# Attention scores with the array's row halves on two heads of a pair, queries turned once, keys and values in plain order

## The chip, the core and the metric

The kernel runs on one core of a Trainium2 chip. The metric is device time in microseconds. TensorE is called PE below; its weight loads are the rows PEld. DVE is VectorE, ACT is ScalarE, POOL is GpSimd, and SP is the queue that issues nearly all DMAs.

## The reference

What matters here is the attention part; two feed-forward blocks on its result follow.

```python
def _attn_ref(q, k, v, w1, b1, w2):          # batch 2, heads 8, seq 576, head_dim 64, all float32
    scores = scale * np.matmul(q, k.transpose(0, 1, 3, 2))
    ...
    h = np.maximum(x @ w1 + b1, 0.0)         # x: a function of the two positions
    bias = h @ w2                            # one number for each head and pair of positions
    scores = scores + bias.transpose(2, 0, 1)[None, :, :, :]
    attn = np.exp(scores - np.max(scores, axis=-1, keepdims=True))
    attn = attn / (np.sum(attn, axis=-1, keepdims=True) + 1e-09)
    return np.matmul(attn, v)
```

## The kernel before

The queries of both batches are cut into nine tiles of 128 rows (`TILES`; the seventh, `COMB`, holds the last 64 rows of both batches). A tile has four pairs of heads, so that there are 36 units u = 4t + p, and the attention part is a pipeline over these 36 units. For each unit:

- `scores` (line 442, written S.u in the table) multiplies the turned queries by the turned keys. A head has only 64 dimensions, so one product fills 64 of the array's 128 rows. Before the change the lower 64 rows take the even keys of a head and the upper 64 rows its odd keys. For this the raw keys are loaded as pairs of neighbouring rows (512 bytes in one piece), and the queries are loaded twice into the two halves of a tile, so that each turned tile of queries holds the same head in both halves.
- `softmax_d` (line 455, on DVE) adds the bias and takes the row's extreme; it writes the tile `e` with the keys back in plain order, which is a step of two elements. `softmax_a` (line 466, on ACT) takes the exponential.
- `e_turn` (T.u.0 to T.u.2) turns `e` on PE, 128 columns at a time, nine times in a unit, into the PSUM tile `tps`; eight of the nine read every second column (`e[:, o:o + 255:2]`), the ninth reads 128 columns in a row. `e_copy` brings the result to SBUF on ACT or DVE.
- `pv` (PV.u, line 504) multiplies by the values.

Ahead of and between these stand the turning of keys (kT) and queries (`q_turn`, qT.t.0 and qT.t.1: four transposes each into `qps`, then `q_copy` on ACT) and the bias groups (B.n). A bias group is made of `bias_R` (R, mostly on DVE), `bias_mm` (`bps`, PE), `bias_evac` (`ev`, ACT and DVE), `bias_store` to DRAM (`biasd`), and later `bias_load` back into the tile `bias`. Weights of the feed-forward part come as `raw`, are converted by ACT (line 145) and DVE (lines 153, 154, 158) in `wm`, split into `wh` and `wl` (lines 137 and 166), and wait there for their use.

PE's order in this part is the written table `ORDER`. The order on the other engines and on the DMA queue is chosen by the scheduler when the kernel is built; it follows the planner's keys and the space that is free in SBUF. Each engine and the queue of SP run in order: an instruction that waits holds back all that stand behind it. PSUM has two buffers for scores (`ps_s`) and three for everything that is turned (`ps_t`).

Of the kernel before, what the change touches and what calls it, by code (L numbers as in the profile page):

```python
# [10 lines left out]
F32 = mybir.dt.float32  # L11
F32R = mybir.dt.float32r
I32 = mybir.dt.int32
ACTF = mybir.ActivationFunctionType
# [25 lines left out]
kT.0,0,0 B.16 B.17 B.18 kT.0,1,0 B.19 kT.0,2,0 qT.0.0 B.21 B.22 B.23 B.20 S.0 B.13 B.12 B.11 B.10 B.9 qT.0.1 kT.0,1,1  # L40
B.8 kT.0,0,1 qT.1.0 S.1 T.0.0 B.14 T.0.2 S.2 kT.1,0,0 T.1.0 T.0.1 kT.1,0,1 B.15 T.1.2 S.3 T.1.1 T.2.0 kT.1,1,0 B.24
kT.1,1,1 T.2.2 S.4 T.2.1 PV.0 PV.1 B.25 T.3.0 T.3.2 S.5 PV.2 qT.2.0 qT.1.1 B.26 T.3.1 T.4.0 rps.0 T.4.2 S.6 B.27 B.28
PV.3 T.4.1 T.5.0 T.5.2 S.7 PV.4 T.5.1 T.6.0 T.6.2 S.8 PV.5 B.29 B.30 qT.3.0 T.7.0 qT.2.1 T.7.2 T.6.1 S.9 PV.6 T.7.1
T.8.0 rps.1 T.8.2 S.10 T.8.1 B.32 B.31 PV.7 T.9.0 B.33 PV.8 T.9.1 T.9.2 S.11 T.10.0 T.10.2 S.12 T.11.0 qT.3.1 qT.4.0
B.34 PV.9 T.10.1 T.11.2 S.13 PV.10 B.35 T.11.1 T.12.0 B.0 rps.2 T.12.2 T.13.0 S.14 PV.11 T.12.1 T.13.2 S.15 T.14.0
T.14.2 B.2 B.1 PV.12 T.14.1 T.13.1 S.16 PV.13 B.3 T.15.0 qT.5.0 qT.4.1 T.15.2 S.17 B.4 PV.14 T.15.1 T.16.0 rps.3
T.16.2 S.18 B.5 PV.15 T.16.1 T.17.0 T.17.2 S.19 PV.16 T.17.1 T.18.0 B.7 T.18.2 B.6 S.20 PV.17 T.19.0 qT.6.0 qT.5.1
T.18.1 T.19.2 S.21 PV.18 T.19.1 T.20.0 rps.4 T.20.2 S.22 PV.19 T.20.1 T.21.0 T.21.2 S.23 PV.20 T.21.1 T.22.0 T.22.2
S.24 PV.21 T.22.1 T.23.0 qT.7.0 qT.6.1 T.23.2 S.25 PV.22 T.23.1 T.24.0 rps.5 T.24.2 S.26 PV.23 T.24.1 T.25.0 T.25.2
S.27 PV.24 T.25.1 T.26.0 T.26.2 S.28 PV.25 T.26.1 T.27.0 qT.8.0 qT.7.1 T.27.2 S.29 PV.26 T.27.1 T.28.0 rps.6 T.28.2  # L50
S.30 PV.27 T.28.1 T.29.0 T.29.2 S.31 PV.28 T.29.1 T.30.1 T.31.0 T.30.0 T.30.2 S.32 PV.29 qT.8.1 T.31.2 S.33 PV.30
# [14 lines left out]
def kernel(ctx, tc, q, k, v, w1, b1, w2, w_in, w_out, w_gate, w_val, w_out2, rms_g, dtab, ntab, itab, out):  # L66
# [170 lines left out]
    if True:  # L237
# [27 lines left out]
        kS = [p.tile([128, H, SH], F32, name=f"kS{b}") for b, p in enumerate((kp0, kp1))]  # L265
        vs = [p.tile([128, 2, H, 2, D], F32, name=f"vs{b}") for b, p in enumerate((vp0, vp1))]
# [7 lines left out]
        pairs = lambda x: x.rearrange("h (p r) d -> p h (r d)", r=2)  # L274

        def load_q(t, hh):

            if hh == 0:
                raw_t["q", t] = rawp.tile([128, H, 2, D], F32, tag="rawq", name="rawq", bufs=BUFS["rawq"])
            h = slice(4 * hh, 4 * hh + 4)  # L280
            for z in range(2):
                a = raw_t["q", t][:, h, z, :]
                if t == COMB:
                    for b in range(B):
                        nc.sync.dma_start(out=a[64 * b:64 * b + 64], in_=q[b, h, 512:576, :].rearrange("h s d -> s h d"))
                else:
                    b, c = TILES[t]
                    nc.sync.dma_start(out=a, in_=q[b, h, c * 128:(c + 1) * 128, :].rearrange("h s d -> s h d"))

        def load_k(b, blk, hh):  # L290

            a = rawp.tile([128, 4, 2, D], F32, tag="rawk", name="rawk", bufs=BUFS["rawk"])
            if blk == 2:
                for o in range(4):
                    src = k[o // 2, 4 * (o % 2):4 * (o % 2) + 4, 512:576, :]
                    nc.sync.dma_start(out=a[32 * o:32 * o + 32].rearrange("p h r d -> p h (r d)"), in_=pairs(src))
            else:
                nc.sync.dma_start(out=a.rearrange("p h r d -> p h (r d)"), in_=pairs(k[b, 4 * hh:4 * hh + 4, 256 * blk:256 * blk + 256, :]))
            raw_t["k", b, blk, hh] = a
# [13 lines left out]
        def turn_four(a, name):  # L313
            ps = ps_t.tile([128, 4, 128], F32, tag="t", name=name)
            for x in range(4):
                transpose(ps[:, x, :], a[:, x].rearrange("p z d -> p (z d)"))
# [619 lines left out]
```

## Time and profile before

| | |
|---|---|
| median of three runs (lowest, highest) | 646.02 us (645.57, 646.43) |
| span of the profiled execution | 646.5 us |
| attention part, from the start to the first `h` matmul of the feed-forward part | 210.5 us |
| feed-forward part | 436.0 us |
| PE busy over the span | 623.6 us (96%) |
| DVE busy | 460.9 us (71%) |
| ACT busy | 340.9 us (53%) |
| mean granted clock of PE | 0.997 |

The profiled execution has no row outside its span, and the span is as long as the slowest of the three runs (0.1 us apart); so its rows can be read against a time of 646.5 us, 0.5 us over the median.

### The profile page before, as it was taken

How to read it: one execution, taken by the hardware profiler on the slowest of the kernel's cores; microseconds unless marked ns; L12 is line 12 of the kernel's file. 1: busy time of each engine (PE TensorE's matmuls, PEld its weight loads, DVE VectorE, ACT ScalarE, POOL GpSimd, SP SyncE). 2: the span in 40 equal slices, each digit the busy share in tenths (PEclk: the TensorE clock that was granted, in tenths of full speed). 3: DMA queues.
4: the chain of work that ended last, by engine and by line, in shares of the span. 5: the costliest groups of instructions: out<-in, count | busy, mean ns of one | idle time of the engine just before them, and what ended most of it. 6: DMA issues, size and time to landing. Idle time of an engine off the chain costs nothing.

```text
span 646.5 us, 10976 instructions
## 1 busy us (share of the span) xinstructions
PE 623.6 (96%) x4172; PEld 527.6 (82%) x4172; DVE 460.9 (71%) x852; ACT 340.9 (53%) x700; POOL 143.8 (22%) x114
## 2 busy tenths in 40 slices
PE   4889999998999999999999999999999999999997
PEld 2346666676688999999999989999899999999996
DVE  6887788646764899888843799969776761387812
ACT  4867676776766555555534556564444441253511
POOL 1000111001210243333310023323332330033400
PEclk9999999998999999999999999999999999999999
DMA  6899647478500254433320123433434340154301
GB/s 161 273 316 279 178 144 187 116 154 248 200 2 1 71 158 132 131 121 122 119 62 1 34 98 131 131 130 99 138 123 127 103 152 11 34 179 147 98 0 50
DMA packets 74721, 80.16 MB, mean 124 GB/s; under 512 B 23980, under 2 KB 59436, under 8 KB 74668
## 3 DMA queue, kind: packets, MB, share of 16 engines
q1 hardware_dynamic: 74404, 79.38, 41.6%
q8 instruction: 33, 0.54, 0.3%
q14 instruction: 20, 0.16, 0.1%
q10 hardware_dynamic: 264, 0.07, 0.0%
HBM read 66.19 MB, written 13.25 MB: 123 GB/s over the span
## 4 chain that ended last, share of the span: by engine, by line
PE 86%; DVE 5%; DMA 4%; ACT 3%; issue 1%; SPq 0%; ACTq 0%; DVEq 0%
PE h L726 39%; PE ya L771 18%; PE yb L771 9%; PE pv L504 5%; PE tps L101 5%; PE s L442 4%; PE bps L372 3%; DVE e L455 2%; DVE R L359 1%; ACT e L466 1%; DMA raw<-in_moe_w_in_dram 1%; DMA bias<-biasd 1%; ACT ev L395 1%; DMA biasd<-ev 1%; PE qps L101 1%
## 5 line engine op out<-in xcount | busy, mean ns | idle before, releaser
L166 POOL TENSOR_TENSOR wl<-wm,wh 128x512 fp32r<-128x512 f32 x85 | 125.9, 1481 | 305.3 <-ACT wh L137 187.6
L158 DVE SCALAR_TENSOR_TENSOR wm<-raw,wm 128x512 int32<-128x512 int32 x85 | 121.7, 1431 | 1.0
L735 ACT CAST gh<-r 128x384 fp32r<-128x384 f32 x84 | 43.2, 514 | 115.9 <-DVE r L758 69.0
L726 PE MATMUL h<-nh,wh 128*128 128x384 f32 x288 | 97.3, 338 | 0.0
L726 PE MATMUL h<-nh,wl 128*128 128x384 f32 x288 | 96.7, 336 | 0.0
L726 PE MATMUL h<-nl,wh 128*128 128x384 f32 x288 | 96.5, 335 | 0.0
L466 ACT ACTIVATE e<-e,m 128x576 f32<-128x576 f32 x72 | 55.5, 771 | 35.2 <-DVE m L455 35.0
L726 PE MATMUL h<-xh,wh 128*128 128x384 f32 x192 | 65.4, 340 | 0.0
L758 DVE TENSOR_TENSOR r<-r,h 128x384 f32<-128x384 f32 x36 | 19.9, 553 | 63.2 <-PE h L726 63.2
L726 PE MATMUL h<-xh,wl 128*128 128x384 f32 x192 | 64.7, 337 | 0.0
L726 PE MATMUL h<-xl,wh 128*128 128x384 f32 x192 | 64.5, 336 | 0.0
L154 DVE SCALAR_TENSOR_TENSOR wm<-raw,wm 128x512 int32<-128x512 int32 x85 | 60.3, 710 | 2.8
L455 DVE CUSTOM_DVE_ANT_1 e<-s,bias 128x576 f32<-128x576 f32 x72 | 52.4, 757 | 10.4 <-PE s L442 7.9
L145 ACT ACTIVATE wm<-raw 128x512 f32<-128x512 f32 x85 | 57.0, 671 | 3.4 <-DMA raw<-in_moe_w_in_dram 2.7
L738 DVE TENSOR_TENSOR gl<-r,gh 128x384 fp32r<-128x384 f32 x84 | 46.6, 555 | 16.8 <-ACT gh L735 16.8
L726 PEld LDWEIGHTS h<-nh,wh 128*128 128x128 f32 x288 | 54.1, 188 | 2.3 <-DVE nl L835 0.9
L726 PEld LDWEIGHTS h<-nl,wh 128*128 128x128 f32 x288 | 54.1, 188 | 1.4
L359 DVE TENSOR_SCALAR R<-T,NB 128x320 f32<-128x320 f32 (+17 forms) x124 | 49.9, 457 | 7.2 <-PE bps L372 7.0
L101 PE MATMUL tps<-ident,e 128*128 128x128 f32 x324 | 53.0, 297 | 1.7 <-ACT et L486 1.2
L726 PEld LDWEIGHTS h<-nh,wl 128*128 128x128 f32 x288 | 54.0, 188 | 0.0
L101 PEld LDWEIGHTS tps<-ident,e 128*128 128x128 f32 x324 | 41.5, 201 | 14.2 <-issue 6.9
L746 ACT ACTIVATE r<-h,half_c 128x384 f32<-128x384 f32 x48 | 27.7, 577 | 47.7 <-PE h L726 47.7
(95 smaller groups left out, 1092.3 us busy)
## 6 DMA issues: line engine op xcount, KB each, us to landing
raw<-in_moe_w_out_dram SPq DMA_DIRECT2D x33, 512.0 KB, 3.6
biasd<-ev SPq DMA_DIRECT2D x36, 295.5 KB, 3.5
raw<-in_moe_w_in_dram SPq DMA_DIRECT2D x18, 512.0 KB, 3.7
raw<-in_moe_w_gate_dram SPq DMA_DIRECT2D x18, 512.0 KB, 3.6
bias<-biasd SPq DMA_DIRECT2D x15, 576.0 KB, 4.9
raw<-in_moe_w_val_dram SPq DMA_DIRECT2D x16, 512.0 KB, 3.6
rawq<-in_q_dram SPq DMA_DIRECT2D x32, 128.0 KB, 4.1
bias<-biasd SPq DMA_DIRECT2D x10, 288.0 KB, 3.8
```

Of the source, the lines that this page charges most:

```text
L101: nc.tensor.transpose(out, in_, ident[:n, :n])
L145: nc.scalar.activation(out=m, in_=raw[:, :, 1].bitcast(F32), func=ACTF.Abs, scale=2.0 ** -112)
L154: nc.vector.scalar_tensor_tensor(out=m, in0=raw[:, :, 0], scalar=29, in1=m, op0=ALU.logical_shift_right, op1=ALU.bitwise_or,)
L158: nc.vector.scalar_tensor_tensor(out=m, in0=raw[:, :, 1], scalar=-0x80000000, in1=m, op0=ALU.bitwise_and, op1=ALU.bitwise_or,)
L166: nc.gpsimd.tensor_tensor(out=lo, in0=m, in1=hi, op=ALU.subtract)
L359: nc.vector.tensor_scalar(out=R, in0=src, scalar1=NB1[:, col], scalar2=None, op0=ALU.max)
L455: nc.vector.tensor_tensor_reduce(out=e_t[u][:, a, :].rearrange("p (j r) -> p r j", r=2), in0=s[:, :, :SH], in1=bt[u][:, a, :].rearrange("p ...
L466: nc.scalar.activation(out=e_t[u][:, a, :], in_=e_t[u][:, a, :], func=ACTF.Exp, scale=-1.0, bias=m_t[t][:, h:h + 1], accum_out=sum_t[t][:, ...
L726: nc.tensor.matmul(ps, lhsT=w[wz][:, c * 128:(c + 1) * 128], rhs=x[xz][:, c, :], start=(i == 0), stop=(i == 11),)
L735: nc.scalar.copy(out=gh, in_=g)
L738: nc.vector.tensor_tensor(out=gl, in0=g, in1=gh, op=ALU.subtract)
L771: nc.tensor.matmul(y_t[ph, n, t], lhsT=g[gz][:, t * 128:(t + 1) * 128], rhs=w[wz], start=(f == 0 and i == 0), stop=(f == F - 1 and i == 2),)
```

## The change

- Scores: the lower 64 rows of the array take the first head of a pair, the upper 64 rows the second; each product covers the first or the second half of the keys (z). The four products of a unit now run over z first and over the two heads inside, so that both score buffers are taken from the start and each is complete only with the third and fourth product.
- Queries: one load of 256 KB and one `q_turn` of four transposes for a tile in place of four loads of 128 KB and two turns of four.
- Keys and values: loaded in plain order, in pieces of 256 bytes in place of 512, with twice as many DMAs for the large blocks.
- `e` is written and read in plain order: all transposes of `e_turn` read 128 columns in a row.
- `ORDER` loses qT.t.1 for each tile; all that is left keeps its place. The planner's numbers stay.

```diff
-T.14.2 B.2 B.1 PV.12 T.14.1 T.13.1 S.16 PV.13 B.3 T.15.0 qT.5.0 qT.4.1 T.15.2 S.17 B.4 PV.14 T.15.1 T.16.0 rps.3
+T.14.2 B.2 B.1 PV.12 T.14.1 T.13.1 S.16 PV.13 B.3 T.15.0 qT.5 T.15.2 S.17 B.4 PV.14 T.15.1 T.16.0 rps.3
...
-        kS = [p.tile([128, H, SH], F32, name=f"kS{b}") for b, p in enumerate((kp0, kp1))]
-        vs = [p.tile([128, 2, H, 2, D], F32, name=f"vs{b}") for b, p in enumerate((vp0, vp1))]
+        kS = [p.tile([128, 4, S], F32, name=f"kS{b}") for b, p in enumerate((kp0, kp1))]
+        vs = [p.tile([128, 4, H, D], F32, name=f"vs{b}") for b, p in enumerate((vp0, vp1))]
...
+        def load_q(t):
+
+            a = raw_t["q", t] = rawp.tile([128, H, D], F32, tag="rawq", name="rawq", bufs=BUFS["rawq"])
+            if t == COMB:
+                for b in range(B):
+                    nc.sync.dma_start(out=a[64 * b:64 * b + 64], in_=rows(q[b, :, 512:576, :]))
+            else:
+                b, c = TILES[t]
+                nc.sync.dma_start(out=a, in_=rows(q[b, :, c * 128:(c + 1) * 128, :]))
...
-                nc.sync.dma_start(out=a.rearrange("p h r d -> p h (r d)"), in_=pairs(k[b, 4 * hh:4 * hh + 4, 256 * blk:256 * blk + 256, :]))
+                a = rawp.tile([128, 2, 4, D], F32, tag="rawk", name="rawk", bufs=BUFS["rawk"])
+                for c in range(2):
+                    r0 = 256 * blk + 128 * c
+                    nc.sync.dma_start(out=a[:, c], in_=rows(k[b, 4 * hh:4 * hh + 4, r0:r0 + 128, :]))
...
-                for blk in range(2):
-                    r0 = 64 * o + 256 * blk
-                    nc.sync.dma_start(out=vs[b][:, blk, o::2].rearrange("p h r d -> p h (r d)"), in_=pairs(v[b, o::2, r0:r0 + 256, :]))
+                for x in range(4):
+                    r0 = 64 * o + 128 * x
+                    nc.sync.dma_start(out=vs[b][:, x, o::2], in_=rows(v[b, o::2, r0:r0 + 128, :]))
...
-        def q_turn(t, hh):
-            ps_of["q", t, hh] = turn_four(raw_t["q", t][:, 4 * hh:4 * hh + 4], "qps")
-
-        def q_copy(t, hh):
-            if hh == 0:
-                q_t[t] = [qp.tile([128, 4, 128], F32, tag=f"q{z}", name=f"q{z}") for z in range(2)]
-            nc.scalar.activation(out=q_t[t][hh], in_=ps_of["q", t, hh], func=ACTF.Copy, scale=0.125)
+        def q_turn(t):
+            ps_of["q", t] = turn_four(raw_t["q", t], "qps")
+
+        def q_copy(t):
+            q_t[t] = qp.tile([128, 4, 128], F32, tag="q", name="q")
+            nc.scalar.activation(out=q_t[t], in_=ps_of["q", t], func=ACTF.Copy, scale=0.125)
...
             for a in range(2):
-                h = 2 * p + a
-                s = ps_s.tile([128, 2, 512], F32, tag="s", name="s")
+                ps_of["s", u, a] = ps_s.tile([128, 2, 512], F32, tag="s", name="s")
+            for z in range(2):
                 for b, sl in cols:
-                    for r in range(2):
-                        rows = slice(64 * r, 64 * r + 64)
+                    for a in range(2):
+                        half = slice(64 * a, 64 * a + 64)
                         nc.tensor.matmul(
-                            s[sl, r, :SH], lhsT=q_t[t][h // 4][rows, h % 4, sl], rhs=kS[b][rows, h, :], start=True, stop=True,
+                            ps_of["s", u, a][sl, z, :SH], lhsT=q_t[t][half, p, sl], rhs=kS[b][half, p, z * SH:z * SH + SH],
+                            start=True, stop=True,
                         )
...
-                out=e_t[u][:, a, :].rearrange("p (j r) -> p r j", r=2),
+                out=e_t[u][:, a, :].rearrange("p (z j) -> p z j", z=2),
...
-                o = (0, 640, 512)[part] + 256 * (x // 2) + x % 2
-                transpose(ps[:, x, :], e[:, o:o + 128] if part == 2 else e[:, o:o + 255:2])
+                o = (0, 640, 512)[part] + 128 * x
+                transpose(ps[:, x, :], e[:, o:o + 128])
...
-                            lhsT, rhs = vs[b][:, x // 2, 2 * p + a, x % 2, :], et[:, 4 * a + x, sl]
+                            lhsT, rhs = vs[b][:, x, 2 * p + a, :], et[:, 4 * a + x, sl]
```

How the built program moves, at three places. First PE between the scores S.8 and S.9 (`qps` are turned queries, `tps` turned `e`). Before:

```order
L372 MATMUL bps<-R,W2b 32x480 x4
L372 MATMUL bps<-R,W2b 32x496 x4
L101 MATMUL qps<-ident,rawq 128x128 x4
L101 MATMUL tps<-ident,e 128x128 x4
L101 MATMUL qps<-ident,rawq 128x128 x4
L101 MATMUL tps<-ident,e 128x128 x5
L442 MATMUL s<-kS_136,q_787 128x288 x4
```

PE in the changed kernel at the same place:

```order
L370 MATMUL bps<-R,W2b 32x480 x4
L370 MATMUL bps<-R,W2b 32x496 x4
L101 MATMUL qps<-ident,rawq 128x128 x4
L101 MATMUL tps<-ident,e 128x128 x9
L440 MATMUL s<-kS_136,q 128x288 x4
```

One group of four query transposes is gone, and nothing else has moved on PE, here or elsewhere in the program.

Second DVE after the softmax step of u = 8 (the ISA rows are `softmax_d`; R makes bias rows). Before:

```order
L359 TENSOR_SCALAR R<-T,NB_114 128x528 x4
L393 TENSOR_SCALAR ev<-bps,INV 128x95
L359 TENSOR_SCALAR R<-T,NB_114 128x544
L486 COPY et<-tps 128x128
L359 TENSOR_SCALAR R<-T,NB_114 128x544 x2
L455 ISA e,m<-s,bias 128x2x288
```

DVE in the changed kernel at the same place:

```order
L357 TENSOR_SCALAR R<-T,NB_114 128x528 x4
L153 TENSOR_SCALAR wm<-wm 128x512
L391 TENSOR_SCALAR ev<-bps,INV 128x95
L154 SCALAR_TENSOR_TENSOR wm<-raw,wm 128x512
L484 COPY et<-tps 128x128
L357 TENSOR_SCALAR R<-T,NB_114 128x544 x3
L158 SCALAR_TENSOR_TENSOR wm<-raw,wm 128x512
L453 ISA e,m<-s,bias 128x576
```

The conversion of the first feed-forward weight now stands here, and those of the next two stand within the two units that follow (u = 9 and 10); before, the first four stood around u = 24 to 28, and the changed kernel has its fourth at u = 22. Their `raw` loads on SP and their first step on ACT (line 145) have moved with them: the smaller query tiles leave room in SBUF, so that the scheduler can place `raw` and `wm` before the bias tiles are freed.

Third SP at the first bias loads (`bias` is what the first softmax steps wait for; `rawk` are keys). Before:

```order
L401 DMA biasd_71<-ev 16x8x591 x2
L427 DMA bias<-biasd_72 128x576 x2
L427 DMA bias<-biasd_72 128x2x576
L298 DMA rawk<-in_k_dram 128x4x128
L427 DMA bias<-biasd_72 128x2x576 x2
```

SP in the changed kernel at the same place:

```order
L399 DMA biasd_71<-ev 16x8x591 x2
L425 DMA bias<-biasd_72 128x576
L296 DMA rawk<-in_k_dram 128x4x64 x2
L425 DMA bias<-biasd_72 128x576
L425 DMA bias<-biasd_72 128x2x576 x3
```

A block of keys, now in two DMAs, stands ahead of the second half of the bias for u = 0 and of the bias for u = 1; it stood behind both.

## Rows read from the trace of the kernel before

**Rows 1.** Busy time by stage: us, PE, PEld, DVE, ACT, POOL, clock, DMA share, GB/s.

```profile
0.00:42.00 42.00, 28.26 (x211) 12.62 (x213) 30.72 (x88) 26.62 (x60) 2.33 (x13) 1.00 0.85 245
42.00:85.00 43.00, 42.25 (x405) 28.43 (x401) 34.76 (x91) 31.64 (x73) 2.70 (x3) 1.00 0.80 215
85.00:104.00 19.00, 18.91 (x198) 12.48 (x196) 14.83 (x40) 13.59 (x30) 2.09 (x2) 1.00 0.72 202
104.00:147.00 43.00, 42.96 (x437) 30.43 (x437) 28.68 (x77) 30.63 (x70) 4.06 (x5) 1.00 0.60 141
147.00:180.00 33.00, 29.57 (x366) 22.52 (x363) 23.52 (x53) 22.98 (x53) 7.38 (x7) 0.95 0.69 213
180.00:210.50 30.50, 30.50 (x336) 24.64 (x334) 16.28 (x43) 18.93 (x44) 3.17 (x3) 1.00 0.00 1
210.50:646.50 436.00, 431.19 (x2232) 396.49 (x2232) 312.13 (x465) 196.47 (x374) 122.11 (x82) 1.00 0.32 100
```

**Rows 2.** Chain that ended last, by line: 85 to 105 us, then 147 to 178 us.

```profile
by line: DVE R L359 16.2%; ACT ev L395 13.8%; ACT e L466 11.9%; DMA rawq<-in_q_dram 10.4%; DVE e L455 10.0%; issue 6.6%; DVE et L486 6.0%; PE bps L372 5.5%; ACT q L340 5.4%; PE s L442 3.8%; SPq L401 2.6%; DVE ev L393 2.5%; ACT rt L528 2.2%;
...
by line: DMA raw<-in_moe_w_in_dram 21.7%; DVE e L455 11.8%; PE s L442 9.1%; PE pv L504 8.2%; ACT e L466 8.1%; DVE wm L154 7.5%; issue 5.1%; PE tps L101 4.8%; DVE et L486 4.5%; PE qps L101 4.2%; DVE wm L158 4.2%; DVE wm L153 3.3%; ACT et L48
```

**Rows 3.** PE timeline: start us, us, operation, count (`qps` queries, `tps` turned `e`).

```profile
54.67 1.09 PE L101 MATMUL qps<-ident,rawq 128*128 128x128 f32 x8
...
121.64 1.22 PE L101 MATMUL tps<-ident,e 128*128 128x128 f32 x8
```

**Rows 4.** Line 101 alone: count, ns min/median/max, first and last start.

```profile
L101 PEld LDWEIGHTS tps<-ident,e x324: 138/209/219, 32.0 to 208.1; 128*128 128x128 f32 x162
L101 PEld LDWEIGHTS qps<-ident,rawq x72: 137/141/153, 15.0 to 191.8; 128*128 128x128 f32 x72
L101 PE MATMUL qps<-ident,rawq x72: 272/273/329, 15.1 to 191.9; 128*128 128x128 f32 x72
```

**Rows 5.** Chain at the start (a DMA), and DVE's first wait for u = 1 (timeline).

```profile
27.62 6.32 DMA bias<-biasd
...
34.07 0.76 DVE L455 CUSTOM_DVE_ANT_1 e<-s,bias 128x576 f32<-128x576 f32 x1 [1.55 <-DMA bias<-biasd]
```

**Rows 6.** Stretches of value loads, then query loads: us, POOL, clock, DMA share, GB/s.

```profile
45.00:47.00 2.00, 0.04 (x1) 1.00 1.12 261
...
51.00:53.00 2.00, 0.00 (x0) 1.00 1.05 197
```

**Rows 7.** Chain (first row) and timeline, 146 to 161 us, around the first `raw` load.

```profile
146.01 6.72 DMA raw<-in_moe_w_in_dram
...
149.80 1.20 PE L442 MATMUL s<-kS,q 64*64 64x288 f32 x16
...
150.94 1.09 PE L504 MATMUL pv<-et,vs 128*64 128x128 f32 x16
...
152.91 0.69 ACT L145 ACTIVATE wm<-raw 128x512 f32<-128x512 f32 x1 [2.73 <-DMA raw<-in_moe_w_in_dram]
...
156.16 0.66 PE L101 MATMUL qps<-ident,rawq 128*128 128x128 f32 x4 [2.32 <-ACT et L486]
...
156.91 1.71 PE L442 MATMUL s<-kS,q 64*64 64x288 f32 x16
...
158.54 1.97 PE L504 MATMUL pv<-et,vs 128*64 128x128 f32 x16
```

**Rows 8.** DVE: two steps of a weight's conversion (timeline), and its busy time 72 to 96 us.

```profile
153.63 0.43 DVE L153 TENSOR_SCALAR wm<-wm 128x512 int32<-128x512 int32 x1 [2.28 <-ACT wm L145]
...
155.37 0.69 DVE L158 SCALAR_TENSOR_TENSOR wm<-raw,wm 128x512 int32<-128x512 int32 x1
...
72.00:96.00 24.00, 18.71 (x49) 1.00 0.47 132
```

**Rows 9.** Timeline: exponential of u = 17, and the turning that reads it.

```profile
120.60 0.76 ACT L466 ACTIVATE e<-e,m 128x576 f32<-128x576 f32 x1
...
126.76 1.33 PE L101 MATMUL tps<-ident,e 128*128 128x128 f32 x9
```

More of the change, by code (lines that the diff above doesn't have):

```diff
@@ L39 @@
 ORDER = """
[L40 to L44, printed above, removed]
+kT.0,0,0 B.16 B.17 B.18 kT.0,1,0 B.19 kT.0,2,0 qT.0 B.21 B.22 B.23 B.20 S.0 B.13 B.12 B.11 B.10 B.9 kT.0,1,1
@@ L271 @@
         copy = lambda e: {"A": nc.scalar.copy, "D": nc.vector.tensor_copy, "P": nc.gpsimd.tensor_copy}[e]
-        pairs = lambda x: x.rearrange("h (p r) d -> p h (r d)", r=2)
-        def load_q(t, hh):
-            if hh == 0:
[L279 to L288, printed above, removed]
+        rows = lambda x: x.rearrange("h s d -> s h d")
@@ L293, in load_k @@
             if blk == 2:
-                for o in range(4):
-                    src = k[o // 2, 4 * (o % 2):4 * (o % 2) + 4, 512:576, :]
-                    nc.sync.dma_start(out=a[32 * o:32 * o + 32].rearrange("p h r d -> p h (r d)"), in_=pairs(src))
-            else:
-                nc.sync.dma_start(out=a.rearrange("p h r d -> p h (r d)"), in_=pairs(k[b, 4 * hh:4 * hh + 4, 256 * blk:256 * blk + 256, :]))
+                a = rawp.tile([128, H, D], F32, tag="rawk", name="rawk", bufs=BUFS["rawk"])
@@ L299, in load_k @@
+                for o in range(2):
+                    nc.sync.dma_start(out=a[64 * o:64 * o + 64], in_=rows(k[o, :, 512:576, :]))
+            else:
+                a = rawp.tile([128, 2, 4, D], F32, tag="rawk", name="rawk", bufs=BUFS["rawk"])
+                for c in range(2):
+                    r0 = 256 * blk + 128 * c
+                    nc.sync.dma_start(out=a[:, c], in_=rows(k[b, 4 * hh:4 * hh + 4, r0:r0 + 128, :]))
+                a = a.rearrange("p c h d -> p (c h) d")
             raw_t["k", b, blk, hh] = a
@@ L315, in turn_four @@
             for x in range(4):
-                transpose(ps[:, x, :], a[:, x].rearrange("p z d -> p (z d)"))
+                transpose(ps[:, x, :], a[:, 2 * x:2 * x + 2].rearrange("p h d -> p (h d)"))
             return ps
@@ L612 @@
         at(P["lv1"], ("lv", 1), (), load_v, 1)
-        QK = {(0, 0): P["q0"], (0, 1): P["q1"], (1, 0): P["q2"], (1, 1): P["q3"]}
+        QK = {0: P["q0"], 1: P["q2"]}
         for t in range(NT):
-            for hh in range(2):
-                at(-97 + hh if t == 0 else (P["lq1"] if t == 1 else 4 * (t - 1) + P["lq"]) + .001 * hh, ("lq", t, hh), (), load_q, t, hh)
-                w = "z" if (t, hh) == (0, 0) else ""
-                key = QK.get((t, hh), 4 * (t - 1) + (P["qa"], P["qb"])[hh])
-                at(key, ("qT", t, hh), [("lq", t, hh)], q_turn, t, hh)
-                at(key + P[w + "qh"], ("qP", t, hh), [("qT", t, hh)], q_copy, t, hh)
+            at(-97 if t == 0 else P["lq1"] if t == 1 else 4 * (t - 1) + P["lq"], ("lq", t), (), load_q, t)
+            key = QK.get(t, 4 * (t - 1) + P["qa"])
+            at(key, ("qT", t), [("lq", t)], q_turn, t)
+            at(key + P["zqh" if t == 0 else "qh"], ("qP", t), [("qT", t)], q_copy, t)
         for u in range(NU):
@@ L626 @@
             ks += [("kC", (0, 2, 0), b) for b in range(B)]
-            at(u + P["s0"], ("S", u), ks + [("qP", t, p // 2)], scores, u)
+            at(u + P["s0"], ("S", u), ks + [("qP", t)], scores, u)
             for a in range(2):
```

27 lines of the change are left out of this document (14 added, 13 removed).

## The prediction

> **What bounds the kernel now.** I read the busy time by stage first [rows 1]. The feed-forward part, from 210.5 us on, has PE busy for 431 of 436 us and contains none of the changed code, so the change is decided in the first 210.5 us. There the reader is to see three kinds of stage. Until 42 us PE idles for 13.7 us; bias groups, their trip to DRAM and the DMAs set the pace (DMA share 0.85). From 42 to 147 us and from 180 us on PE is busy for 99% of the time: less work on PE is less time. Between 147 and 180 us PE idles for 3.4 us, and the granted clock falls to a mean of 0.95. Then the chain of waits [rows 2], because "busy" also holds short stalls inside a run of matmuls. Between 85 and 105 us its leading entries are R on DVE, ev and e on ACT; between 147 and 178 us the load of a weight, e on DVE and the conversion wm. So in 52 of the 168 us after the start (85 to 104 and 147 to 180) PE is full, or nearly, but others run level with it.
>
> **Query turns.** Each tile loses one group of four transposes. Eight query transposes after another kind of work take 1.09 us [rows 3]; without the first one's 0.329 us [rows 4] that is 0.76 us for seven, 0.109 each, 0.44 for four. Nine groups are 3.9 us. One of them stands in the start, where PE waits anyway: 3.5 us count. The nine copies that ACT loses, and the halved bytes of the query loads, count nothing by themselves, since neither is what PE waits for in the full stages.
>
> **Transposes of e.** 36 units have eight transposes each that now read their 128 columns in a row. In the trace the weight load of a turned e, most of which read every second column, has a median of 209 ns; the query's, in a row, has 141 ns, and the shortest of e, 138, is like it [rows 4]. How much of these 68 ns shows? Eight of e take 1.22 us, eight of a query 1.09 us, both after another kind of work [rows 3]: 0.13 us for eight, the rest lies under the matmuls. Over the 34 units after the start this is 4.5 us. The bounds are 0, if it isn't the step that makes the load long, and 9.4 us, if each group of four (72 of them) pays 0.13. I take 4.5, which is the like-for-like row.
>
> The Trainium skill speaks against this term: SBUF — State Buffer, section "Door 1: The DMA port swizzle", says that consecutive accesses to a 16-byte line run at full bandwidth, so that a stride costs nothing up to four fp32. By that rule a step of two elements is free and the term is 0; the row's 209 against 141 ns does not agree with it.
>
> **What PE saves.** 3.5 and 4.5 are 8.0 us, spread over 168 us. In the 52 us where others run level I let half of it through: 8.0 x 52/168 x 1/2 = 1.2 us is lost. 6.8 us remain.
>
> **The order of the scores.** The first head's scores are complete after the third product, not the second: DVE gets them up to half of a unit's products later, 0.6 us of 1.20 [rows 7]. I cost it at nothing. The exponential of u = 17 is over at 121.4 us, and the run of nine that holds its turning starts at 126.8 [rows 9]: some 5 us of cover. Queued behind the waiting DVE instruction are copies of et and bias rows, which PE needs for its three turning buffers; were the cover gone, it would be 0.6 us for each unit, 22 us in all.
>
> **Keys and values in smaller pieces.** The trace has both sizes: while values in 512-byte pieces came, 261 GB/s at a share of 1.12, which is 233 for a full share; while queries in 256-byte pieces came, 197 at 1.05, which is 188 [rows 6]. The keys and values that are loaded after the first units' keys are 3.7 MB: 15.9 us of all DMA engines become 19.7, 3.8 more; 0.5 MB of queries that are not loaded twice in this stretch give 2.7 back. What waits is the bias of u = 1: its load took 6.3 us, and DVE idled 1.55 us until it [rows 5]. On SP a block of keys (0.25 MB, 1.4 us at 188 GB/s) now stands ahead of it, and that block waits for a turning on PE first. DVE has its next bias rows ahead of this wait now, which refunds some. I take +1.0 us; the bounds are +3.8 (the whole extra DMA time on the path) and -0.5 (the query turn of the start shows after all).
>
> **Weights, converted earlier.** This is what the diff doesn't say. The first three weights are loaded and converted around u = 8 to 10 (68 to 95 us before) in place of u = 24 to 28. Given back between 147 and 180 us: there ACT waited 2.73 us for the first raw load, PE 2.32 us behind it, and then PE ran slowly: scores 1.71 in place of 1.20 us, values 1.97 in place of 1.09 [rows 7]. With the stage's 3.4 us of idle time [rows 1] that makes 3.4 + 0.5 + 0.9 = 4.8 us. Paid at the new place, two things. ACT's first step again waits for a raw load; the DMAs are about to go quiet there, so I take 1.2 us, between 0 and the 3.7 us (2.3 idle, 1.4 slow) that it cost before. And DVE: each conversion is 0.43 + 0.69 + 0.69 us, three are 5.4 us, and DVE has 5.3 us free between 72 and 96 us [rows 8], with nothing to spare. PE's cover for a late DVE is the 5 us above and the turning buffers; I take 2.4 us, near the middle of 0 and 5.4. Net -1.2 us, between -4.8 and +4.3.
>
> **Sum.** -6.8 + 1.0 - 1.2 = -7.0 us against the profiled 646.5, 639.5. The median of the runs stands 0.5 us lower: 639.0 us.
>
> **Rivals.**
> A, the forecast: PE's saving shows, moved weights and start nearly cancel. 639.0, own range 636 to 643.
> B, nothing is paid: all 8.0 us of PE, 4.8 us back between 147 and 180 us, start and new place of the weights free: 646.0 - 12.8 = 633.2, range 632 to 636. For it: DMA share falls after 70 us, and the bias rows made early on DVE. Against it: the full DVE.
> C, the weights' new place takes over, the end on the other side. ACT waits the whole 6.7 us of a raw load's landing [rows 7], with evacuations of the bias and et copies queued behind it, PE then runs slowly for a while (1.4 us), and DVE's 5.4 us all show: 13.5 us in place of 3.6, so 648.9; range 644 to 650. It decides from 10.6 us paid between 65 and 110 us. For it: 85 to 105 us is already led by DVE and ACT [rows 2]. Against it: the loads' bytes meet a quieter DMA than at 146 us.
> D, the step doesn't matter: the long weight loads of e come from something else, and the second term is nil. Of 4.5 us 3.8 had been let through: 642.8. For it: most of the 68 ns is hidden even now. Against it: the shortest loads of e. The Trainium skill's rule on 16-byte lines, named above, would be this case.
>
> **How the numbers follow.** A measurement of this kernel can tell about 0.2%, 1.3 us, from no change. Chances: A 0.50, B 0.20, C 0.20, D 0.10. The range 633.5 to 646.0 holds A and D, the upper half of B and the lower part of C, about 0.8. Faster (under 644.7): A, B, 0.09 of D and 0.03 of C, 0.82. Same: 0.01 of D and 0.08 of C, 0.09. Slower: 0.09 of C.
>
> **What would show it.** Right: 36 rows of qps in place of 72; weight loads of tps at about 141 ns, and eight tps in some 1.09 us; the first h matmul near 203 us; no idle PE and a full clock between 140 and 175 us; the feed-forward part 436 us as before. ACT's first wait for raw near 70 us with under 3 us, and PE idle for 1 to 4 us between 65 and 100. DVE's first e for u = 1 within 1 to 2 us of 34 us. Wrong: tps loads still at 209 ns (D); PE idle for over 10 us between 65 and 110 (C); PV.0 or qT.2 waiting for DMAs near 50 us, which would mean that the smaller pieces cost more than the rows say; DVE waiting for scores in unit after unit with PE idle behind it, which would mean that the order of the scores was not covered.

## The result and the profile after

The changed kernel takes 651.07 us (median of six runs, 649.78 to 652.46) against 645.99 us (median of six, 645.57 to 648.34): a ratio of 1.0073, with a 95% interval from 1.0059 to 1.0088. It is 4.7 us slower, where 639.0 us, 7 us faster, had been forecast. The profiled execution has a span of 648.0 us in a run of 649.78; a run's time stands some 1.8 us above its span, so the span of 646.5 on which the sum was built is not that of a run of 646.43, as was assumed, but of one of about 648.3, like the highest of the runs before (648.34). The forecast of 639.0 is still 7.0 under the median, but its rows come from an execution some 2 us slower than most.

Busy time by stage of the changed kernel, in the columns of [rows 1]; attention now ends at 212 us:

```profile
0.00:42.00 42.00, 26.81 (x201) 11.58 (x201) 31.38 (x90) 25.98 (x58) 2.34 (x13) 0.96 0.86 232
42.00:85.00 43.00, 37.31 (x356) 24.27 (x348) 33.12 (x83) 29.43 (x69) 2.71 (x3) 1.00 0.90 252
85.00:104.00 19.00, 17.55 (x191) 11.38 (x191) 16.50 (x42) 11.72 (x26) 2.09 (x2) 1.00 0.59 186
104.00:147.00 43.00, 42.27 (x433) 27.42 (x430) 29.21 (x79) 30.87 (x69) 5.36 (x6) 1.00 0.50 133
147.00:180.00 33.00, 30.78 (x404) 23.22 (x403) 21.77 (x52) 21.75 (x53) 6.17 (x6) 1.00 0.47 129
180.00:212.00 32.00, 30.91 (x337) 24.22 (x337) 16.39 (x45) 19.08 (x47) 3.15 (x3) 1.00 0.01 2
212.00:648.00 436.00, 431.21 (x2233) 396.51 (x2232) 312.18 (x465) 196.81 (x374) 121.53 (x82) 1.00 0.32 100
```

PE is busy for 616.8 us in place of 623.6: the 6.8 us that the forecast let through are there. But they came out as idle time. Between 42 and 85 us PE now idles for 5.7 us (0.75 before, [rows 1]), between 85 and 104 for 1.5 (0.1), and in the last stage, which had none, for 1.1. Over the whole attention part PE idles for 26.4 us, 8.3 more than before. The feed-forward part is the same. The first `h` matmul, forecast near 203 us, comes at 212.

The granted clock of PE fell to the lower of its two levels (1.2 GHz) once in the attention part of each profiled execution, but at different places: before near 157 us, behind a wait of PE of 2.32 us [rows 7], and in the changed kernel in the start, behind a stretch in which PE had been busy for 0.90 of 3 us (first row before, the others changed):

```profile
157.00:160.00 3.00, 3.00 (x30) 1.96 (x32) 2.59 (x7) 3.00 (x8) 1.28 (x1) 0.58 0.87 241
...
30.00:33.00 3.00, 0.90 (x4) 0.45 (x6) 2.52 (x8) 1.29 (x4) 0.00 (x0) 1.00 1.00 335
33.00:37.00 4.00, 4.00 (x19) 1.68 (x19) 2.14 (x5) 2.37 (x7) 0.00 (x0) 0.57 0.99 296
```

So the clock is full between 140 and 175 us, as forecast, but the stretch is not saved: it stands elsewhere. The clock also goes with the differences between the changed kernel's runs: the three shortest (649.78 to 650.72 us) have a mean granted clock of 0.996 to 0.997, the three longest (651.42 to 652.46) one of 0.991 to 0.992.

Line 101 of the changed kernel, and one run of eight (first two rows as [rows 4], third as [rows 3]):

```profile
L101 PEld LDWEIGHTS tps<-ident,e x324: 137/140/231, 34.5 to 209.7; 128*128 128x128 f32 x162
...
L101 PEld LDWEIGHTS qps<-ident,rawq x36: 138/141/143, 14.6 to 176.6; 128*128 128x128 f32 x36
...
58.80 1.09 PE L101 MATMUL tps<-ident,e 128*128 128x128 f32 x8
```

Both savings on PE are there as forecast: 36 query transposes fewer, loads of e at 140 ns in place of 209, eight of e in 1.09 us in place of 1.22. Also as forecast are the wait of DVE for the bias of u = 1, no longer than in [rows 5], and ACT's first wait for `raw`, at its new place and shorter than in [rows 7] (timeline):

```profile
33.97 0.76 DVE L453 CUSTOM_DVE_ANT_0 e<-s,bias 128x576 f32<-128x576 f32 x1 [1.17 <-DMA bias<-biasd]
...
75.77 0.67 ACT L145 ACTIVATE wm<-raw 128x512 f32<-128x512 f32 x1 [1.33 <-DMA raw<-in_moe_w_in_dram]
```

So the loss is in what had been costed at little. The prediction had named two signs of this. The first: qT.2 waiting for DMAs near 50 us. Here it is (PE, then SP's queue, timeline):

```profile
57.38 0.63 PE L101 MATMUL qps<-ident,rawq 128*128 128x128 f32 x4 [1.65 <-DMA rawq<-in_q_dram]
...
40.58 2.67 SPq L305 DMA_DIRECT2D vs<-in_v_dram  x4
...
43.98 3.22 SPq L305 DMA_DIRECT2D vs<-in_v_dram  x4
...
47.92 2.52 SPq L305 DMA_DIRECT2D vs<-in_v_dram  x4
...
51.17 2.25 SPq L305 DMA_DIRECT2D vs<-in_v_dram  x4
...
54.12 0.60 SPq L284 DMA_DIRECT2D rawq<-in_q_dram  x1
```

The queries of the third tile stand behind 20 DMAs of values and are issued at 54.12 us; in the kernel before, the first of their loads was issued at 49.58 us, after half as many large loads:

```profile
40.05 1.17 SPq L306 DMA_DIRECT2D vs<-in_v_dram  x2
...
42.03 1.61 SPq L306 DMA_DIRECT2D vs<-in_v_dram  x2
...
49.58 2.91 SPq L288 DMA_DIRECT2D rawq<-in_q_dram  x4
```

The second sign: DVE waiting for scores in unit after unit. Idle time by what ended it, 85 to 205 us (us in total, times, longest); the kernel before:

```profile
DVE e L455 <- PE s L442: 7.0, 14, 2.1
ACT e L466 <- DVE m L455: 22.7, 24, 2.2
PEld tps L101 <- ACT et L486: 1.1, 2, 0.8
```

and the changed one:

```profile
DVE e L453 <- PE s L440: 13.9, 19, 2.3
ACT e L464 <- DVE m L453: 35.7, 25, 2.2
PEld tps L101 <- ACT et L484: 6.2, 10, 1.6
PE tps L101 <- ACT et L484: 3.3, 8, 1.4
```

DVE waits twice as long for scores, ACT 13 us longer for DVE, and PE's weight loads for turnings of e wait for copies of et at ten places in place of two.

### The profile page after: what moved, and what is told of

Same layout as the page of the kernel before. It is cut to its first block, busy times and chain, and to the rows that moved or that the text cites. A ratio compares the mean times of both kernels' runs of the same rounds, so it can differ in the third digit from the quotient of the medians.

```text
span 648.0 us, 10847 instructions
## 1 busy us (share of the span) xinstructions
PE 616.8 (95%) x4136; PEld 518.6 (80%) x4136; DVE 460.6 (71%) x852; ACT 335.6 (52%) x691; POOL 143.3 (22%) x114
## 4 chain that ended last, share of the span: by engine, by line
PE 80%; ACT 5%; DVE 4%; DMA 4%; SPq 3%; issue 2%; POOL 0%; ACTq 0%; POOLq 0%; DVEq 0%
PE h L722 39%; PE ya L767 18%; PE yb L767 9%; PE s L440 5%; PE pv L502 3%; PE tps L101 3%; ACT e L464 3%; PE bps L370 2%; DVE e L453 2%; SPq L305 1%; DVE R L357 1%; ACT ev L393 1%; DMA rawq<-in_q_dram 1%; DMA raw<-in_moe_w_out_dram 1%; ACT et L484 1%
## 5 line engine op out<-in xcount | busy, mean ns | idle before, releaser
L101 PE MATMUL tps<-ident,e 128*128 128x128 f32 x324 | 49.3, 284 | 7.1 <-ACT et L484 4.1
L101 PEld LDWEIGHTS tps<-ident,e 128*128 128x128 f32 x324 | 35.6, 142 | 22.6 <-ACT et L484 7.5
L137 ACT CAST wh<-wm 128x512 fp32r<-128x512 f32 x85 | 52.3, 618 | 1.0 <-DVE wm L158 0.9
```

Source lines behind the costliest of these rows:

```text
L101: nc.tensor.transpose(out, in_, ident[:n, :n])
L137: nc.scalar.copy(out=hi, in_=m)
```

## The experiments

A per cent of the kernel before is 6.46 us. Ratios are to the kernel before, run on the same chip; a difference of two ratios has an uncertainty of 0.2 to 0.3%, 1.1 to 2 us.

**The two suspects, each alone on the kernel before.** First the order of the products:

```diff
-            for a in range(2):
-                ...
-                    for r in range(2):
+            for z in range(2):
+                ...
+                    for a in range(2):
+                        h, r = 2 * p + a, (a + z) % 2
```

> The kernel before with one thing changed: a unit's four products take the two score buffers in turn (first head's odd or even keys, second head's, first's, second's), as in the change; loads, turnings, keys and weights stay. Theory 'order' (the order of the scores, costed at nothing, is the largest cost: a unit needs both score buffers free before its first product, and the first softmax step starts 0.6 us later): +5 to +9 us over the kernel before, with DVE's wait for scores up from 10.4 us towards 16 us and PE waiting for DVE's m and for et in the stages from 85 us on. Theory 'pieces' (the smaller DMA pieces of keys and values are the cost): within 1 us of the kernel before. Theory 'weights' (the earlier conversion is the cost): within 1 us of the kernel before.

Measured: 1.0092 (1.0076 to 1.0108), 5.9 us slower. The order of the scores alone costs more than the whole loss, and not through the clock: the granted clock is 0.997 to 1.000 in these runs and in those of the kernel before beside them. Then the pieces:

```diff
+                for r in range(2):
+                    r0 = 256 * blk + r
+                    nc.sync.dma_start(out=a[:, :, r, :], in_=k[b, 4 * hh:4 * hh + 4, r0:r0 + 255:2, :]...)
```

> The kernel before with keys and values loaded in pieces of 256 bytes, two DMAs for each one of before; all else stays, the order of PE to the row. Theory 'pieces': +3 to +6 us over the kernel before, with PE waiting between 28 and 62 us for the bias of the first units and for raw queries, and u = 9 starting 3 to 4 us later. Theory 'order': 0 to +2 us. The forecast had +1.0, between -0.5 and +3.8.

Measured: 1.0191 (1.0170 to 1.0212), 12.3 us slower, twice the most that had been expected. One wait is longer than all of it (PE, then SP's queue):

```profile
44.29 1.08 PE L101 MATMUL qps<-ident,rawq 128*128 128x128 f32 x4 [13.40 <-DMA rawq<-in_q_dram]
...
36.56 6.00 SPq L288 DMA_DIRECT2D rawq<-in_q_dram  x4
```

The four query loads of the second tile came behind the doubled key loads. In the changed kernel there is one load for this tile, and it stands near the start of the queue, issued before 10 us, so this wait does not exist there. So the 12.3 us are no measure of what the pieces cost in the changed kernel.

**The other way round: each undone in the changed kernel.**

```diff
-                for x in range(4):
-                    nc.sync.dma_start(out=vs[b][:, x, o::2], in_=rows(v[b, o::2, r0:r0 + 128, :]))
+                for blk in range(2):
+                    nc.sync.dma_start(out=half[:, o::2], in_=pairs(v[b, o::2, r0:r0 + 256, :]))
```

> The changed kernel with keys and values loaded in pieces of 512 bytes and half as many DMAs, as before the change; the data then stand in other places, so that the output is not the reference's; all work stays. Theory 'pieces' in the changed kernel: qT.2's wait of 1.65 us for its raw queries near 57 us goes, the first units start 1 to 3 us earlier, and the time is 2 to 5 us under the changed kernel (646 to 649). If the cost is in the order of the scores: within 1 us of the changed kernel (650 to 652).

Measured: 0.9999 (0.9989 to 1.0009). The pieces cost 0.74%, 4.8 us. A part of this may come with the clock: eight of these ten runs have a mean granted clock of 0.997 or more, the changed kernel's six 0.991 to 0.997. The two profiled executions, at 0.999 and 0.997, are 3.9 us apart (spans of 644.1 and 648.0).

```diff
-            for z in range(2):
+            for a in range(2):
                 for b, sl in cols:
-                    for a in range(2):
-                        half = slice(64 * a, 64 * a + 64)
+                    for z in range(2):
+                        half = slice(64 * z, 64 * z + 64)
```

> The changed kernel with the four products of a unit in the order of before (first head's buffer with both row halves, then the second's); the two heads are then mixed, so that the output is not the reference's; the work stays. Theory 'order': the cost that the edit brought alone to the kernel before (6.1 us) comes back, 5 to 7 us under the changed kernel (644 to 646). If the cost overlaps with that of the pieces: 2 to 4 us. If the two add up badly only in the kernel before: under 1 us.

Measured: 0.9978 (0.9965 to 0.9991). The order costs 0.95%, 6.1 us, as it did alone.

> The changed kernel with both edits undone, the pieces of 512 bytes and the order of the scores (output not the reference's); what is left of the change is PE's saving and the weights' new place. If the forecast's terms for these are right: 646.0 - 6.8 - 1.2, about 638, between 636 and 641. If PE's saving is eaten by the other engines in any case: 643 to 646.

Measured: 0.9897 (0.9880 to 0.9913), 6.7 us faster than the kernel before. The two costs add up (11.4 us together, 4.8 and 6.1 apart), and what is left of the change is close to what had been forecast for it.

**The terms that remain.** The step of the transposes, first in the changed kernel:

```diff
-                o = (0, 640, 512)[part] + 128 * x
-                transpose(ps[:, x, :], e[:, o:o + 128])
+                o = (0, 640, 512)[part] + 256 * (x // 2) + x % 2
+                transpose(ps[:, x, :], e[:, o:o + 128] if part == 2 else e[:, o:o + 255:2])
```

> The changed kernel with the transposes of e reading every second column again, as before the change (the softmax is then multiplied with values in another order, so the output is not the reference's); the order of instructions on every engine stays to the row. If the step sets the length of the weight load and its cost shows: weight loads of tps at a median near 209 ns, eight tps at 1.22 us, and 3 to 5 us over the changed kernel (the forecast's term was 4.5). If the saving was eaten because other engines set the pace: loads at 209 ns, and within 1.5 us of the changed kernel. If the step is not what makes the loads long: loads at 142 ns, no change.

Measured: 1.0102 (1.0087 to 1.0117), 0.29% or 1.9 us over the changed kernel. Then where nothing else stands in the way:

> The changed kernel with the pieces of 512 bytes and the order of the scores both undone, as in the run where only PE's saving and the weights' new place were left (6.7 us under the kernel before), and now with every second column read by the transposes of e again, too (output not the reference's); the order of instructions is that of the former run to the row. If the forecast's term for the step (4.5, of which 3.8 let through) is right: 642 to 645, 3 to 5 us above the former run. If the step's cost is mostly hidden: within 1.5 us of it, and then the query turns and the weights' place are worth more than forecast. In the changed kernel itself the step cost only some 2 us.

Measured: 0.9940 (0.9919 to 0.9962), 0.43% or 2.8 us over the run without the step. Line 101 without and with the step, all else being equal to the row:

```profile
L101 PEld LDWEIGHTS tps<-ident,e x324: 137/140/144, 33.4 to 199.9; 128*128 128x128 f32 x162
```

```profile
L101 PEld LDWEIGHTS tps<-ident,e x324: 137/209/219, 32.8 to 204.1; 128*128 128x128 f32 x162
```

So the step makes the load long (209 against 140 ns), and rival D is out. The Trainium skill's rule that the prediction weighed (SBUF — State Buffer, "Door 1: The DMA port swizzle") would have made this difference nil; 140 against 209 ns decide against it for weight loads.

The place of the weights:

```diff
-            a = raw_t["q", t] = rawp.tile([128, H, D], F32, tag="rawq", ...)
+            a = rawp.tile([128, 2 * H, D], F32, tag="rawq", ...)[:, :H, :]
...
-            q_t[t] = qp.tile([128, 4, 128], F32, tag="q", name="q")
+            q_t[t] = qp.tile([128, 8, 128], F32, tag="q", name="q")[:, :4, :]
```

> The changed kernel with the raw and the turned query tiles padded to their former size in SBUF, so that the first weights are loaded and converted around u = 24 to 28 again, as before the change; nothing is computed otherwise. Theory 'weights' (the early conversion costs more at 65 to 110 us than it gives back at 147 to 180): 3 to 8 us faster than the changed kernel, at 643 to 648 us. Theories 'order' and 'pieces': the stall at 146 to 160 us comes back, and the time is 0 to 5 us over the changed kernel, 651 to 656. The forecast's own terms (paid 3.6, regained 4.8) give +1.2 over the changed kernel.

Measured: 1.0099 (1.0076 to 1.0121), 0.26% or 1.7 us over the changed kernel, no more than the uncertainty. So the early conversion gives back about what it costs, or somewhat more; rival C, by which it had to cost 8.7 us net, is out.

**How the pieces cost it.** The query loads moved ahead of half of the values by a planner's number (`lq` from -2.569 to -3.2, `lq1` from -0.018 to -0.4):

> The changed kernel with one of its planner's numbers lowered, so that the query loads stand earlier in SP's queue: those of the third tile ahead of the second batch's values. The computation is the reference's. If qT.2's wait for its load (1.65 us near 57 us) is on the path: 1 to 2 us under the changed kernel (649 to 650). If DVE and ACT set the pace there: within 0.7 us of it.

Measured: 1.0037 (1.0023 to 1.0051), 2.3 us back. The place of the loss agrees: against the run with the large pieces, the changed kernel's scores start 1.6 us later at u = 2, between whose scores and those of u = 1 the stretch at the lower clock lies, 2.8 us at u = 6, behind the wait for the third tile's queries, 3.6 at u = 9, and 4.0 us in all units from u = 12 on. Then fewer DMAs with small pieces:

```diff
-                for x in range(4):
-                    nc.sync.dma_start(out=vs[b][:, x, o::2], in_=rows(v[b, o::2, r0:r0 + 128, :]))
+                for x in (2 * o, 2 * o + 1):
+                    nc.sync.dma_start(out=vs[b][:, x], in_=rows(v[b, :, 128 * x:128 * x + 128, :]))
```

> The changed kernel with pieces of 256 bytes kept and half as many DMAs for the large blocks of keys and values (each brings all eight heads of 128 rows, 256 KB; the data then stand in other places, so that the output is not the reference's). The order of PE, DVE, ACT and POOL stays to the row. If the number of DMAs on SP's queue (some 0.6 us each) is what the pieces cost: 3 to 5 us under the changed kernel (646 to 648), as with the pieces of 512 bytes. If the size of the pieces costs it: within 1 us of the changed kernel (650 to 652).

Measured: 1.0044 (1.0027 to 1.0061). Neither expectation holds alone: the number of DMAs is worth 0.29%, 1.9 us, of the 4.8, and 2.9 us stay with the size of the pieces, with an uncertainty of 1.4 us on this division. SP's queue in this run, to be read beside the eight loads of before and the 16 of the changed kernel:

```profile
41.60 1.28 SPq L303 DMA_DIRECT2D vs<-in_v_dram  x2
...
44.66 1.23 SPq L303 DMA_DIRECT2D vs<-in_v_dram  x2
```

The stretches in which the values come, in the columns of [rows 1], first in the changed kernel, then in this run:

```profile
42.00:54.00 12.00, 11.14 (x113) 7.42 (x107) 9.38 (x26) 8.33 (x22) 0.66 (x1) 1.00 0.84 192
...
42.00:52.00 10.00, 9.14 (x68) 5.26 (x62) 8.07 (x20) 5.63 (x15) 0.65 (x1) 0.83 1.02 202
```

In the changed kernel the DMA engines are not full (share 0.84): 16 loads of 128 KB at 0.67 us each on SP (10.66 us, above) are 197 GB/s, an estimate near the 192 that the row has, which speaks for SP's issuing as what sets the pace there. With half as many DMAs the share is 1.02, and 202 GB/s is what the small pieces allow. Either limit alone leaves the other close behind it.

Values off SP's queue (`nc.gpsimd.dma_start` for the 16 large loads):

> The changed kernel with the 16 large loads of values issued by POOL's queue in place of SP's; pieces and numbers stay, and the computation is the reference's. POOL has little to do and issues them in the first microseconds, when the loads for the first units and the bias need the DMAs too. If SP's queue is what costs in the pieces and the DMAs have room: 2 to 5 us under the changed kernel. If the values take the DMAs from the bias of the first units: 1 to 6 us over it, with the start of u = 1 and 2 later by as much.

Measured: 1.0150 (1.0123 to 1.0178), 5 us slower than the changed kernel: POOL issues ten of them between 7.6 and 15.1 us, and the first scores of u = 1 start at 37.6 us in place of 30.8. The second expectation holds: issued this early, the values delay the first units. What SP's queue costs later, where the values come in the changed kernel, this run does not tell.

**How the order costs it.** It makes the first softmax step late, and it makes PE need both score buffers. The second alone, on the kernel before:

```diff
-            for a in range(2):
+            for a in ((0, 1), (1, 0))[u % 2]:
                 ps_of["s", u, a] = ps_s.tile([128, 2, 512], F32, tag="s", name="s")
```

> The kernel before with the score buffers taken in turn by units: in every second unit the first head's scores go into the buffer that the softmax frees last. The order of the products, and of every instruction on every engine, stays as before; only the buffer in which a head's scores stand changes, so that PE must wait for both softmax steps of the former unit before its first product, while the first head is complete with the second product as before. The computation is the reference's. If the need for both buffers is what the order of the scores costs: 4 to 6 us over the kernel before. If the lateness of the softmax is the cost: within 1 us of it.

Measured: 1.0005 (0.9990 to 1.0019), no cost. (By the edit the first head's scores go into the buffer that is freed last in every unit from u = 1 on, not only in every second; the test is the stronger for it.) Lateness, again on the kernel before (`S.18 B.5 PV.15` becomes `B.5 PV.15 S.18`, and so in 27 units):

> The kernel before with S.u moved behind PV.(u-3) in the table, in 27 of the units: both heads' scores, and with them the softmax, start 1.1 us later against the turnings that read them, and PE asks later for the score buffers. The computation is the reference's. If lateness is the cost of the order of the scores (6.1 us for 0.6 us a unit): 8 to 14 us over the kernel before. If the need for both buffers is the cost: within 1 us of the kernel before, or faster.

Measured: 1.0340 (1.0317 to 1.0363), 22 us slower, 0.8 us for each of 27 units that were 1.1 us late. Not all of it is lateness of the softmax: PV also asks earlier for its et, and 4.7 us of PE's idle time between 85 and 205 us are such waits. But a cover of some 5 us would have hidden most of these 1.1 us, and 0.8 of them show. The waits of this run, as above:

```profile
DVE e L442 <- PE s L429: 18.4, 12, 2.7
ACT e L453 <- DVE m L442: 38.2, 21, 3.2
PEld tps L88 <- ACT et L473: 6.8, 8, 3.1
```

Two attempts to give the changed kernel its cover back, both on top of the earlier query loads. T.u.2 behind T.u.1:

> The changed kernel with the query loads earlier in SP's queue (as in the run before: 2.3 us under the changed kernel) and with each unit's single turning T.u.2 moved behind T.u.1, a unit later in the table, so that PE asks later for the exponential of the second head and for the free turning buffer. The computation is the reference's. If the cost of the order of the scores is the lateness of the softmax, as PE's waits for et at T.u.2 suggest: 2 to 4 us under the version with the query loads alone (644.5 to 646.5). If the cost is that PE must have both score buffers free: within 1 us of that version.

Measured: 1.0098 (1.0062 to 1.0135), 4 us slower than the query loads alone. PE's waits for copies of et at the turnings of e fall from 3.3 to 0.6 us (85 to 205 us), but waits of 2.7 us at a turning of `rps` and of 1.0 us at turnings of queries take their place. That is 1 us more, of the 4; the rest stays open. And S.u one place ahead:

> The changed kernel with the query loads earlier in SP's queue and with S.u moved one place ahead in the table, before T.(u-2).2: the softmax of a unit can begin some 0.3 us earlier, but PE asks for both score buffers 0.3 us earlier. The computation is the reference's. If the lateness of the softmax is the cost: 1 to 4 us under the version with the query loads alone (648.5). If the need for both buffers is the cost: the same as it, or up to 3 us slower.

Measured: 1.0016 (1.0003 to 1.0030), 1.4 us better than the query loads alone, at the edge of what can be told; if it is real, it points to lateness too.

**A version without the two costs.** The kernel before, with the queries loaded and turned once:

```diff
+            nc.scalar.activation(out=q_t[t][0], in_=ps, func=ACTF.Copy, scale=0.125)
+            for z in range(2):
+                lo, hi = slice(64 * z, 64 * z + 64), slice(64 - 64 * z, 128 - 64 * z)
+                nc.gpsimd.tensor_copy(out=q_t[t][1][hi], in_=q_t[t][0][lo])
```

> The kernel before with one part of the change alone: queries loaded once (256 KB) and turned once, as in the change; the second copy that the even and odd keys need is made by two copies of 64 rows on POOL, which shift the rows by 64. Scores, keys, values, pieces and e stay as before. The computation is the reference's. If the two terms that went wrong are the order of the scores and the pieces, this version pays neither: -3.5 for the query turns, -1 to -2 for the weights, which are converted early here too, so 640 to 643. If the copies on POOL arrive late or slow DVE down: 645 to 648.

Measured: 0.9971 (0.9956 to 0.9987), 1.9 us faster than the kernel before and so faster than both kernels, but less than its terms: the run with the step, which differs from it mainly by the shifted copies, had gained 3.9.

> The version with queries loaded and turned once on the kernel before (1.9 us under it) with the shifted copies of the first two tiles on ACT in place of POOL. The computation is the reference's. If POOL's copies in the start are what that version loses against its terms: 641.5 to 643.5, 3 to 4.5 us under the kernel before. If it loses time elsewhere: within 1 us of the former version (643.5 to 645).

Measured: 0.9989 (0.9972 to 1.0007), no better. Where this version loses some 2 us stays open.

## Why the prediction was wrong

By its own terms, forecast against measured:

| term | forecast | measured |
|---|---|---|
| query turns, with the weights' place | -3.5 (before the discount) and -1.2 | -3.9 (the run with the step), of which the weights some -1.7, within the uncertainty |
| transposes of e | -4.5, before the discount | -2.8 without the two faults below, -1.9 in the changed kernel |
| these three, after the discount of 1.2 | -8.0 | -6.7 |
| keys and values in smaller pieces | +1.0, at most +3.8 | +4.8 |
| order of the scores | 0 | +6.1 |

**The step that failed is "The order of the scores".** It said: "I cost it at nothing", with "some 5 us of cover". The cover was measured from the exponential to the turning that reads it [rows 9], and that distance was right. But it is not the wait that closes first. A unit of the changed kernel (timeline):

```profile
156.86 1.20 PE L440 MATMUL s<-kS,q 64*64 64x288 f32 x16
...
158.11 0.76 DVE L453 CUSTOM_DVE_ANT_0 e<-s,bias 128x576 f32<-128x576 f32 x1
...
158.91 0.78 ACT L464 ACTIVATE e<-e,m 128x576 f32<-128x576 f32 x1 [1.27 <-DVE m L453]
...
159.23 1.09 PE L101 MATMUL tps<-ident,e 128*128 128x128 f32 x8
...
159.69 0.76 ACT L464 ACTIVATE e<-e,m 128x576 f32<-128x576 f32 x1
...
160.45 0.56 ACT L484 COPY et<-tps 128x512 f32<-128x512 f32 x1
...
161.06 0.33 PE L101 MATMUL tps<-ident,e 128*128 128x128 f32 x1 [0.30 <-ACT et L484]
161.32 1.20 PE L440 MATMUL s<-kS,q 64*64 64x288 f32 x16
```

The same unit with the order undone:

```profile
155.16 1.20 PE L440 MATMUL s<-kS,q 64*64 64x288 f32 x16
...
155.95 0.76 DVE L453 CUSTOM_DVE_ANT_0 e<-s,bias 128x576 f32<-128x576 f32 x1
...
158.28 1.04 ACT L484 COPY et<-tps 128x512 f32<-128x512 f32 x2
...
158.90 0.32 PE L101 MATMUL tps<-ident,e 128*128 128x128 f32 x1
159.15 1.20 PE L440 MATMUL s<-kS,q 64*64 64x288 f32 x16
```

DVE starts 1.25 us after the scores in place of 0.79; ACT's two exponentials come as much later; the copy of et, of turnings done meanwhile, stands behind them in ACT's queue; PE's next turning needs the PSUM buffer that this copy frees; and the next scores stand behind that turning. The circle takes 4.46 us in place of 3.99: 0.47 more, which is the lateness of DVE (0.46), passed on whole. That closing of the circle through ACT's queue is read from these rows, and no run changed ACT's order to test it; that the buffers for scores alone cost nothing, and that late scores do cost, is what the two experiments showed. Over the last 22 units DVE starts a median of 1.27 us after the scores in place of 0.80. But not every unit pays for it. The scores of u = 27 and 28, first in the changed kernel, then with the order undone:

```profile
169.35 1.20 PE L440 MATMUL s<-kS,q 64*64 64x288 f32 x16
...
172.93 1.24 PE L440 MATMUL s<-kS,q 64*128 64x288 f32 x8
...
166.71 1.20 PE L440 MATMUL s<-kS,q 64*64 64x288 f32 x16
...
170.29 1.24 PE L440 MATMUL s<-kS,q 64*128 64x288 f32 x8
```

Both are 3.58 us apart, though DVE is as late here. `ORDER` tells the two kinds apart. Between S.27 and S.28 stand three turnings, as many as there are buffers for them; between S.24 and S.25, the unit shown above, stands a fourth (qT.7), and the single turning behind it needs the buffer of the first. From u = 18 on, seven units have three turnings before their scores (u = 19, 23, 24, 27, 28, 31, 35), and all are equally long in both traces, to 0.01 us. Nine have a fourth, of queries, of `rps` or of e; eight of them (u = 18, 22, 25, 26, 29, 30, 32, 34) are 0.39 to 0.65 us longer, one (u = 21) is not. (u = 20 and 33 are of neither kind.) From u = 15 on the units add up to 4.6 of the 6.1 us; before that the starts of these two executions differ too much to be compared. The prediction had a price (0.6 a unit; 0.47 was measured, where it is paid) and the two queues, and even wrote that copies of et stand behind the waiting instruction; it then took the cover of another consumer for theirs.

**"Keys and values in smaller pieces" was mis-sized**: 4.8 us in place of 1.0, and 1.0 above its own upper bound, though this last is within the uncertainty. The bound was the longer time on full DMA engines. But SP pays for each DMA that it issues, and the term did not count the DMAs: the loads of values are 16 in place of 8 on a queue behind which the next tile's queries wait, and in the changed kernel the DMA engines are not full while they come (0.84, above). Nor had the term the stretch at the lower clock, 33 to 37 us. The rate for small pieces itself, 188 GB/s for a full share [rows 6], is near what the run with half as many DMAs shows (202 at 1.02, or 198); the changed kernel's own 192 at 0.84 would be 229. By the rows of the prediction (233 and 188) the small pieces take 24% more time for the same bytes, where the engines are full. The Trainium skill (DMA: Bandwidth & Descriptors, "Why small descriptors are slow (HBM only)") gives three cycles for each packet on top of its bytes, by which 512 bytes in two packets would take 22 cycles for 19, an estimate of 16% more; the direction agrees, the rows say more.

**What was right.** The query turns, the step and the weights' place came out at 6.7 us together against 8.0. The step came out at 2.8 us against 4.5 (34 units of 0.13 us are 4.4), of which 3.8 had been let through; with an uncertainty of 1.7 us that is no clear miss. Of the weights, some 1.7 us against 1.2 agrees, but two of its parts were taken from one execution: the slow scores and values behind 0.5 and 0.9 us stand in the stretch at the lower clock, and the traces of the order alone and of the exchanged buffers, which leave the weights where they were, have a full clock all through 147 to 180 us. The conditions that rival C needed were not there: ACT's wait at the new place is 1.33 us, where 1.2 had been taken, and PE idles for 4.2 us between 65 and 110 us, where that rival asked for over 10. The forecast without its two faulty terms, 638.0, stands beside 639.56 us for the kernel that has neither.

## What to carry to other kernels

When an instruction becomes late, the cover is not the distance to the consumer of its result: follow everything that stands behind the late instruction on each engine's queue, and take the shortest way back to the busy engine. Where that way closes on itself within a unit (scores, softmax, a copy behind it, a freed buffer, next scores), lateness is paid in full however empty the other engines look; here that was so in units with one turning more than there are buffers, and not in the others. When a load is cut into more DMAs, count the DMAs on the queue that issues them besides the bytes, and see whose load stands behind them.

## What the hardware showed unexpectedly

Weight loads of 128 columns take 140 ns when the columns stand in a row and 209 ns with a step of two elements, in runs that are otherwise the same to the row. SP takes 0.62 to 0.67 us for each of these DMAs, though bytes and pieces differ by a factor of two: 0.64 for the 256 KB loads in 512-byte pieces (5.15 us for the eight of the kernel before), 0.67 for 128 KB in 256-byte pieces (10.66 us for the 16 of the changed one), 0.62 for 256 KB in 256-byte pieces (4.97 us for eight). POOL copied 64 rows of 512 elements into the other 64 rows in a median of 612 ns.
